# Slot-logit block sums take a turn in the two-buffer PSUM pool of the transposes, and the slot maximum is emitted at the end of its pair

## The chip, the cores and the metric

One core of a Trainium2 chip (eight cores in two dies of four) runs the whole program. The metric is the device time of that core in microseconds, as the median of several executions. Durations inside the program come from one profiled execution.

## The reference, cut to what matters

```python
scores = scale * q @ k.transpose(0, 1, 3, 2)                    # (4, 8, 576, 576)
scores = where((rel >= 0) & (rel < 128), scores + bias, -1e9)   # sliding window
attn = exp(scores - scores.max(-1)); attn /= attn.sum(-1) + 1e-9
x = (attn @ v) as (2304, 512)                                   # tokens x model
logits = x @ phi                                                # (2304, 32 slots)
d = softmax of logits over the tokens; c = softmax of logits over the slots
slot_input = d.T @ x                                            # 8 experts x 4 slots
slot_out = relu(slot_input @ w1) @ w2                           # per expert
x = c @ slot_out                                                # (2304, 512)
h = x @ w_in
out = (h * clip(h + 3, 0, 6) / 6) @ w_out
```

What the change touches is the softmax `d`, which runs over all 2304 tokens: its maximum per slot is a running one, taken block by block while the attention is still being computed.

## The kernel before

The first half, to about 176 us, is the attention stage. Its work is cut into 80 steps (batch 4, tiles of 128 tokens 5, of which the fifth has 64, pairs of heads 4). The loop at line 478 takes two steps, a "pair", at a time and emits, in the order written in `STEP` (line 30), these operations; the schedule is manual, so each engine runs its instructions in the order in which they are emitted:

- `s0 s1` (`do_s`, line 434, and `emit_s`, line 179): loads for later tiles; TensorE's score matmuls into `sp` (L190, two tiles), VectorE's bias, running minimum and row result `st` (L202), ScalarE's exponential in `pb` (L210). `do_s` also issues the loads of `q`, `k`, `v` of later tiles and of the weights on SyncE's queue; from tile 17 on (`m > 16`, line 449) it issues all weight tiles for which a buffer is free, ahead of the next `q`.
- `p0 p1` (`emit_pv`, line 241): for the two steps four back, the matmuls with `v` into `o` (L257). After the fourth step of a tile ScalarE copies `o` to `xt` (L268), and `push_tile` (line 402) appends side work.
- `b0` (`do_b`, line 472): one entry of `turnsq`, below, if it is due.
- `t0` (`emit_t`, line 228): transposes of `pb` into a tile `t` of `ps_t` (L237), two steps back; an even step's tile is copied to `xb` by VectorE, an odd one's by ScalarE (L239).
- `n0` (`emit_norm`, line 214): VectorE's reciprocal of the row sums of this pair (L217, L219) and GpSimd's multiplication of `pb` with it (L224).
- `t1`: the second transposes.
- `x0` (`do_x`, line 468): one entry of `side`: `side_x` (line 270) transposes `xt` into `xps` and ScalarE copies it to `x` (L274, L277); `side_l` (line 279) makes the slot logits `lps` and ScalarE copies them to `el` (L283, L285).

`turnsq` holds, for a block of tokens of one batch (tiles 0-1, 2-3 and 4; in the last batch tiles 0-1 and 2), three entries that are taken one per pair, the first `SLAG` = 3 steps after the block's last tile:

- `side_max` (line 289): a matmul with block identities sums the four partial logits of `el` into `lt` (L296); VectorE's maximum over it (L298) and its negation against the running one (L303); ScalarE's exponential of `lt` back into `el` (L312), the copy of 32 plain rows (L314), the factor by which older sums are rescaled (L316); VectorE's running denominator (L321), which reads that factor. The first block of all has no earlier maximum, and neither L316 nor L321.
- `side_e` (line 325): transposes of `el` into `ln` (L328), ScalarE's copy `e` (L335) and VectorE's copy into `cn` (L336). VectorE's copy is issued with a wait for ScalarE's.
- `side_s` (line 340): matmuls `ss` of `e` with `x` (L345), added to `acc` by VectorE (L351).

PSUM is full: `sp` has four banks, `ps_t` two buffers, `ps_o` one and `ps_m` one. `lt`, `ln`, `ss`, `xps` and `lps` all take that one buffer of `ps_m` in turn, and each must wait until the tile before it has been read by its last reader.

The last tiles of the last batch end differently: `last_l` (line 354) makes their logits in `sp`, and after the loop `last_max` (line 363) does maximum, exponential, transposes (`lnl`) and sums in one go. Then come the two expert products, whose weights stream in, and the second product, all unchanged.

Of the kernel before, what the change touches and what calls it, by code (L numbers as in the profile page):

```python
# [9 lines left out]
F32 = mybir.dt.float32  # L10
# [16 lines left out]
NW, NX, NY, NV, NPB = 9, 10, 2, 4, 4  # L27
LAG_T, LAG_PV = 2, 4
CMOD, CACT = 2, 1
STEP, SLAG = "s0 s1 p0 p1 b0 t0 n0 t1 x0", 3  # L30

CB = NP * 384
CX = CB + 128 + 128 + 128
# [11 lines left out]
def nq(i):  # L45
    return 128 if i < 4 else 64
# [3 lines left out]
def body(ctx: ExitStack, tc, q, k, v, phi, we, wf, cst, sel, out):  # L50
# [78 lines left out]
    with ExitStack() as a:  # L129
# [10 lines left out]
        ps_t = a.enter_context(tc.tile_pool(name="ps_t", bufs=2, space=PSUM))  # L140
        ps_o = a.enter_context(tc.tile_pool(name="ps_o", bufs=1, space=PSUM))
        ps_m = a.enter_context(tc.tile_pool(name="ps_m", bufs=1, space=PSUM))
# [127 lines left out]
        def side_x(b, i):  # L270
            w = nq(i)
            t = ps_m.tile([128, NP, 128], F32, tag="m", name=f"xps{b}_{i}")
            for j in range(NP):
                nc.tensor.transpose(out=t[0:w, j, :], in_=xt[b, i][:, j, 0:w], identity=ident)  # L274
            xn[b, i] = xp.tile([128, DM], F32, tag="x", name=f"x{b}_{i}")
            cp_ = nc.vector.tensor_copy if (b, i) == tiles[-1] else nc.scalar.copy
            cp_(out=xn[b, i][0:w].rearrange("p (j d) -> p j d", j=NP), in_=t[0:w])  # L277

        def side_l(b, i):
            w = nq(i)  # L280
            t = ps_m.tile([128, 128], F32, tag="m", name=f"lps{b}_{i}")
            for j in range(NP):
                nc.tensor.matmul(out=t[32 * j:32 * j + 32, 0:w], lhsT=phi4[:, j, 0],  # L283
                                 rhs=xt[b, i][:, j, 0:w], start=True, stop=True)
            nc.scalar.copy(out=el[:, i * 128:i * 128 + w], in_=t[:, 0:w])  # L285
# [3 lines left out]
        def side_max(b, i0, i1):  # L289
            mx = ep.tile([128, 8], F32, tag="mx", name=f"mx{b}_{i0}")  # L290
            t0, w = 128 * i0, sum(nq(i) for i in range(i0, i1))
            cuts = [(t0, w)] if w <= 512 else [(t0, w // 2), (t0 + w // 2, w // 2)]
            lt = []
            for hh, (c0, cw) in enumerate(cuts):
                t = ps_m.tile([128, 512], F32, tag="m", name=f"lt{b}_{c0}")
                nc.tensor.matmul(out=t[:, 0:cw], lhsT=blk, rhs=el[:, c0:c0 + cw],  # L296
                                 start=True, stop=True)
                nc.vector.reduce_max(out=mx[:, hh:hh + 1], in_=t[:, 0:cw], axis=AX.X)  # L298
                lt.append(t)
            nm = mx[:, 2:3]  # L300
            for hh in range(len(cuts)):
                if hh or run:
                    nc.vector.scalar_tensor_tensor(  # L303
                        out=nm, in0=mx[:, hh:hh + 1], scalar=-1.0, in1=nm if hh else run["nm"],
                        op0=ALU.mult, op1=ALU.min)
                else:
                    nc.vector.tensor_scalar(out=nm, in0=mx[:, 0:1], scalar1=-1.0, scalar2=None,
                                            op0=ALU.mult)
            z = el
            for hh, (c0, cw) in enumerate(cuts):  # L310
                zz = z[:, c0:c0 + cw]
                nc.scalar.activation(out=zz, in_=lt[hh][:, 0:cw], func=AF.Exp, bias=nm,  # L312
                                     accum_out=mx[:, 4 + hh:5 + hh])
                nc.scalar.copy(out=zz[0:32], in_=lt[hh][0:32, 0:cw])  # L314
            if run:
                nc.scalar.activation(out=mx[:, 6:7], in_=run["nm"], func=AF.Exp, bias=nm,  # L316
                                     scale=-1.0)
            if len(cuts) > 1:
                nc.vector.tensor_tensor(out=mx[:, 4:5], in0=mx[:, 4:5], in1=mx[:, 5:6], op=ALU.add)
            if run:  # L320
                nc.vector.scalar_tensor_tensor(out=mx[:, 4:5], in0=run["z"], scalar=mx[:, 6:7],  # L321
                                               in1=mx[:, 4:5], op0=ALU.mult, op1=ALU.add)
            run.update(nm=nm, z=mx[:, 4:5], al=mx[:, 6:7])
# [30 lines left out]
        def last_l(i):  # L354
            c0, w = 128 * (i - 3), nq(i)
            if i == 3:
                run["lg"] = sp[0][:, 0, 0:192]
            for j in range(NP):
                nc.tensor.matmul(out=run["lg"][:, c0:c0 + w],
                                 lhsT=phi4[:, j].rearrange("p g s -> p (g s)"),  # L360
                                 rhs=xt[B - 1, i][:, j, 0:w], start=j == 0, stop=j == NP - 1)
# [38 lines left out]
        side, turnsq = [], []  # L400

        def push_tile(n, b, i):
            if b == B - 1 and i > 2:
                side.append(lambda: last_l(i))
                side.append(lambda: side_x(b, i))
                return
            side.append(lambda: side_x(b, i))
            side.append(lambda: side_l(b, i))
            for i0, i1 in ((0, 2), (2, 3)) if b == B - 1 else ((0, 2), (2, 4), (4, NB)):
                if i == i1 - 1:  # L410
                    for f in (side_max, side_e, side_s):
                        turnsq.append((n + SLAG, lambda f=f, i0=i0, i1=i1: f(b, i0, i1)))

        nc.vector.memset(acc, 0.0)
        warm(ps_m, "m", acc, WARM_0)
# [45 lines left out]
        def do_p(n):  # L461
            m = n - LAG_PV
            if 0 <= m < NSTEP:
                emit_pv(m)
                if steps[m][2] == NP - 1:
                    push_tile(n, *steps[m][:2])
# [2 lines left out]
            if side:  # L469
                side.pop(0)()  # L470

        def do_b(n):
            if turnsq and turnsq[0][0] <= n:
                turnsq.pop(0)[1]()

        ops = {"s": do_s, "t": do_t, "n": do_n, "p": do_p, "x": do_x, "b": do_b}
        with tc.manual_schedule():
            for n in range(0, NSTEP + LAG_PV, 2):
                for c in STEP.split():
                    ops[c[0]](n + int(c[1:]))  # L480
            while turnsq:
                turnsq.pop(0)[1]()
            while side:
                side.pop(0)()
        top.close()
# [13 lines left out]
        t = ps_m.tile([128, NP, 1, NS], F32, tag="m", name="stp")  # L499
# [106 lines left out]
    with ExitStack() as bx:  # L606
# [4 lines left out]
        with tc.manual_schedule():  # L611
# [132 lines left out]
            t = ps_2.tile([128, NP, 128], F32, name="sotp")  # L744
# [66 lines left out]
    def q_out(j):  # L811
        if j < 4:
            nc.scalar.copy(out=qhi[:, j], in_=Q[j])
            nc.vector.tensor_tensor(out=qlo[:, j], in0=Q[j], in1=qhi[:, j].bitcast(F32),
                                    op=ALU.subtract)
            return
        x = tp.tile([128, DM], F32, tag="o", name="qtail")
        nc.vector.tensor_copy(out=x, in_=Q[4])
        return x
# [55 lines left out]
    with tc.manual_schedule(), tc.issue_after(L["last"].ins):  # L875
# [10 lines left out]
        for p in range(8):  # L886
# [9 lines left out]
            if last:  # L896
                x = q_out(4)
# [163 lines left out]
```

## Time and profile before

| what | us |
|---|---|
| three timed runs | 378.14, 378.93, 380.35; median 378.93 |
| the profiled execution, its own time | 379.32 |
| its span, first to last instruction | 377.4 |
| mean granted clock of TensorE (1 is 2.4 GHz) | 0.958 |
| busy: TensorE / VectorE / ScalarE / GpSimd | 336.2 / 192.3 / 178.7 / 82.3 |
| moved by DMA | 71.10 MB, mean 188 GB/s |

How to read what follows. Times are counted from the first instruction. PE is TensorE, DVE VectorE, ACT ScalarE, SPq the queue of SyncE that issues loads. A row of the timeline gives start, length, engine, line, operation and names (written<-read), the number of instructions merged, and in brackets how long the engine idled before and what ended that. A row of the list of waits gives who waited (engine, tile, line), the releaser, the time in total, how often, and the longest. The idle time of an engine counts only where that engine, or one that waits for it, is the last to finish.

### The profile page before, as it was taken

The numbers are of one execution on the slowest core, as the hardware profiler recorded it, in microseconds if no ns is written. First come the engines' busy times: TensorE is split into PE (matmuls) and PEld (weight loads), VectorE is DVE, ScalarE is ACT, GpSimd is POOL, SyncE is SP. The second block draws the span as 40 slices with busy tenths as digits, with TensorE's granted clock in tenths as the row PEclk, the third lists the DMA queues.
The fourth block names the chain that finished last, engine by engine and source line by source line (L and its number), as shares of the span: only waits on it lengthen the run. The fifth ranks groups of instructions, "written<-read, shape, count | busy, mean of one in ns | idle before, by whom it ended". The sixth has DMA issues, their size and how long they took to land. (4 is left out here: it accounts for less than half of the span.)

```text
span 377.4 us, 7557 instructions
## 1 busy us (share of the span) xinstructions
PE 336.2 (89%) x2738; PEld 205.7 (55%) x2738; DVE 192.3 (51%) x617; ACT 178.7 (47%) x551; POOL 82.3 (22%) x182
## 2 busy tenths in 40 slices
PE   6898889897989788687999685999999999999994
PEld 5566556665666556465433131433443358788883
DVE  2655465545555556224200558888888458940000
ACT  3787778777786788242021443222233045632111
POOL 2544254434443344210002200000000011110000
PEclk9999999999999999895899966999999999999999
DMA  8545784559367829177599998762000001122221
GB/s 262 198 168 199 248 325 151 212 209 361 95 215 259 329 76 411 39 240 314 196 423 391 374 425 340 243 219 97 2 0 0 2 2 56 56 83 85 83 82 64
DMA packets 19835, 71.10 MB, mean 188 GB/s; under 512 B 2672, under 2 KB 4848, under 8 KB 13776
## 3 DMA queue, kind: packets, MB, share of 16 engines
q1 hardware_dynamic: 18576, 69.08, 49.1%
q10 hardware_dynamic: 1216, 1.47, 1.2%
q8 instruction: 23, 0.38, 0.4%
q14 instruction: 20, 0.16, 0.1%
HBM read 65.83 MB, written 4.72 MB: 187 GB/s over the span
## 5 line engine op out<-in xcount | busy, mean ns | idle before, releaser
L224 POOL TENSOR_TENSOR pb<-pb,st 128x192 f32<-128x192 f32 (+2 forms) x144 | 63.6, 473 | 98.5 <-DVE st L219 45.2
L210 ACT ACTIVATE pb<-pb,st 128x192 f32<-128x192 f32 (+2 forms) x144 | 61.3, 426 | 24.8 <-DVE st L202 24.8
L805 PE MATMUL q<-F,mf 128*128 128x512 f32 x128 | 62.8, 624 | 4.3 <-DVE mf L793 4.3
L202 DVE CUSTOM_DVE_ANT_0 pb<-sp,cona 128x192 f32<-128x192 f32 (+2 forms) x144 | 40.6, 332 | 28.3 <-PE sp L190 25.8
L838 PE MATMUL acc<-qhi,P 128*128 128x512 f32 x140 | 42.1, 395 | 0.0
L257 PE MATMUL o<-xb,v 128*64 128x128 f32 (+2 forms) x576 | 41.5, 276 | 0.1
L805 PEld LDWEIGHTS q<-F,mf 128*128 128x128 f32 x128 | 23.2, 196 | 33.5 <-issue 22.3
L237 PE MATMUL t<-conp,pb 128*128 128x128 f32 x256 | 39.3, 284 | 2.0 <-POOL pb L224 1.2
L190 PE MATMUL sp<-kt,qz 64*64 64x192 f32 (+2 forms) x576 | 33.6, 318 | 4.9 <-issue 3.6
L257 PEld LDWEIGHTS o<-xb,v 128*64 128x64 f32 (+1 forms) x576 | 30.8, 138 | 12.4 <-issue 7.9
L237 PEld LDWEIGHTS t<-conp,pb 128*128 128x128 f32 x256 | 28.6, 143 | 9.5 <-POOL pb L224 5.8
L838 PEld LDWEIGHTS acc<-qhi,P 128*128 128x128 f32 x140 | 25.9, 188 | 6.1
L210 ACT ACTIVATION_READ_ACCUMULATOR pb<-pb,st 128x1 f32 x144 | 26.9, 187 | 0.0
L239 DVE COPY xb<-t 128x512 f32<-128x512 f32 (+1 forms) x40 | 23.2, 580 | 6.9 <-PE t L237 6.5
L190 PEld LDWEIGHTS sp<-kt,qz 64*64 64x64 f32 x576 | 19.6, 132 | 12.7 <-issue 8.0
L853 ACT ACTIVATE out<-acc 128x512 f32<-128x512 f32 (+1 forms) x18 | 10.6, 586 | 30.9 <-PE acc L838 23.3
L239 ACT COPY xb<-t 128x512 f32<-128x512 f32 (+1 forms) x40 | 19.7, 492 | 7.8 <-PE t L237 7.6
L795 POOL COPY mf<-mt 128x64 f32<-128x64 f32 x8 | 6.2, 774 | 78.2 <-ACT mt L785 53.2
L274 PE MATMUL xps<-conp,xt 128*128 128x128 f32 (+1 forms) x76 | 12.3, 284 | 12.3 <-ACT el L314 8.9
L777 ACT COPY m<-mp 128x256 f32<-128x256 f32 x8 | 3.0, 372 | 41.8 <-PE mp L774 41.8
L838 PE MATMUL acc<-qlo,P 128*128 128x512 f32 x56 | 22.1, 395 | 0.0
L585 DVE TENSOR_TENSOR pf<-R,As 128x512 f32<-128x512 f32 (+1 forms) x20 | 12.7, 637 | 14.1 <-ACT As L569 7.8
(153 smaller groups left out, 453.0 us busy)
## 6 DMA issues: line engine op xcount, KB each, us to landing
w<-in_we_dram SPq DMA_DIRECT2D x30, 1024.0 KB, 6.3
w<-in_wf_dram SPq DMA_DIRECT2D x16, 1024.0 KB, 8.4
out_dram<-out SPq DMA_DIRECT2D x17, 256.0 KB, 2.0
v<-in_v_dram SPq DMA_DIRECT2D x16, 256.0 KB, 3.6
qz<-in_q_dram SPq DMA_DIRECT2D x15, 256.0 KB, 5.2
kt<-in_k_dram SPq DMA_DIRECT2D x15, 256.0 KB, 5.8
kt<-in_we_dram SPq DMA_DIRECT2D x1, 1024.0 KB, 7.2
qz<-in_q_dram SPq DMA_DIRECT2D x6, 128.0 KB, 5.0
```

Source lines behind the costliest of these rows:

```text
L190: nc.tensor.matmul(out=sp[m][64 * e:64 * e + 64, hf, c0:c1], lhsT=qz[64 * u:64 * u + 64, (NB * b + i) % 2, j * w + 64 * hf:j * w + 64 * hf ...
L202: nc.vector.tensor_tensor_reduce(out=p[:, 256 * hf + c0:256 * hf + c1], in0=sp[m][:, hf, c0:c1], in1=bias8[:, j, hf, c0:c1], scale=-0.125, ...
L210: nc.scalar.activation(out=x, in_=x, func=AF.Exp, bias=st[:, 0, r], scale=-1.0, accum_out=st[:, 1, r])
L224: nc.gpsimd.tensor_tensor(out=x, in0=x, in1=st[:, 2, 2 * m + hf:2 * m + hf + 1].to_broadcast([128, c1 - c0]), op=ALU.mult)
L237: nc.tensor.transpose(out=t[:, c, hf], in_=p[:, o:o + 128], identity=ident)
L239: f(out=x[:, p0:2, 0:nh], in_=t[:, p0:2, 0:nh])
L257: nc.tensor.matmul(out=o[64 * u:64 * u + 64, j, 0:w], lhsT=vv[0:kk, 128 * j + 64 * u:128 * j + 64 * u + 64], rhs=y, start=m == 0, stop=m = ...
L274: nc.tensor.transpose(out=t[0:w, j, :], in_=xt[b, i][:, j, 0:w], identity=ident)
L585: nc.vector.tensor_tensor(out=pf, in0=t[:, 0:w], in1=(L["a2"][s % 2] if j == 4 else A[s])[:, 0:w], op=ALU.mult)
L805: nc.tensor.matmul(out=Q[pt], lhsT=mm[p][:, u, 128 * pt:128 * pt + 128], rhs=F[:, u], start=p == u == 0, stop=p == 7 and u == 1)
L838: nc.tensor.matmul(out=acc, lhsT=l, rhs=r[:, j], start=j == 0 and i == 0, stop=j == 4 and i == 1)
L853: nc.scalar.activation(out=o[:, cs], in_=acc[:, cs], func=AF.Copy, scale=1.0 / 6.0))
```

## The change

`lt` is allocated in `ps_t`, the pool of the transposes, with their tag. `STEP` gets a tenth operation, `m0`, behind `x0`. Entries of `turnsq` carry a kind: `side_max` is taken at `m0`, `side_e` and `side_s` at `b0` as before. The list stays one list: an entry is taken only if it is the first and of the kind asked for. Since `m0` comes after `b0` in a pair, a `side_max` can now follow in the pair in which the `side_s` before it was taken.

```diff
-STEP, SLAG = "s0 s1 p0 p1 b0 t0 n0 t1 x0", 3
+STEP, SLAG = "s0 s1 p0 p1 b0 t0 n0 t1 x0 m0", 3
...
-                t = ps_m.tile([128, 512], F32, tag="m", name=f"lt{b}_{c0}")
+                t = ps_t.tile([128, 512], F32, tag="t", name=f"lt{b}_{c0}")
...
-                        turnsq.append((n + SLAG, lambda f=f, i0=i0, i1=i1: f(b, i0, i1)))
+                        turnsq.append((n + SLAG, "m" if f is side_max else "b",
+                                       lambda f=f, i0=i0, i1=i1: f(b, i0, i1)))
...
-        def do_b(n):
-            if turnsq and turnsq[0][0] <= n:
-                turnsq.pop(0)[1]()
+        def do_b(n, kind="b"):
+            if turnsq and turnsq[0][0] <= n and turnsq[0][1] == kind:
+                turnsq.pop(0)[2]()
...
-        ops = {"s": do_s, "t": do_t, "n": do_n, "p": do_p, "x": do_x, "b": do_b}
+        ops = {"s": do_s, "t": do_t, "n": do_n, "p": do_p, "x": do_x, "b": do_b, "m": lambda n: do_b(n, "m")}
...
             while turnsq:
-                turnsq.pop(0)[1]()
+                turnsq.pop(0)[2]()
```

VectorE around the maximum over tiles 2-3 of the second batch, before (`mx` is the maximum, `xb<-t` the copy of a transpose, L217 and L219 the reciprocal, L202 the score reductions, here the next pair's first):

```order
L298 TENSOR_REDUCE mx_2_1270<-lt_256_1271 128x1
L303 SCALAR_TENSOR_TENSOR mx_2_1270<-mx_2_1270,mx_0_1057 128x1
L321 SCALAR_TENSOR_TENSOR mx_2_1270<-mx_0_1057,mx_2_1270 128x1
L239 COPY xb_110<-t_1279 128x256
L217 TENSOR_SCALAR st_1247<-st_1247 128x4
L219 RECIPROCAL st_1247<-st_1247 128x4
L202 ISA pb_112,st_1310<-sp_116,cona 128x192
```

and with the change:

```order
L239 COPY xb_110<-t_1270 128x256
L217 TENSOR_SCALAR st_1247<-st_1247 128x4
L219 RECIPROCAL st_1247<-st_1247 128x4
L298 TENSOR_REDUCE mx_2_1291<-lt_256_1292 128x1
L303 SCALAR_TENSOR_TENSOR mx_2_1291<-mx_2_1291,mx_0_1082 128x1
L321 SCALAR_TENSOR_TENSOR mx_2_1291<-mx_0_1082,mx_2_1291 128x1
L202 ISA pb_112,st_1310<-sp_116,cona 128x192
```

The three instructions of the maximum moved from ahead of the pair's copy and reciprocal to right ahead of the next pair's score reductions.

TensorE at the same place, before (`o` the products with `v`, `xps` the transposes of a finished tile):

```order
L257 MATMUL o_4_1214<-xb_111,v_4_848 64x64 x2
L296 MATMUL lt_256_1271<-el,conp 128x256
L237 MATMUL t_1279<-conp,pb_112 128x128 x2
L237 MATMUL t_1289<-conp,pb_113 128x128 x2
L274 MATMUL xps_4_1293<-conp,xt_4_1268 64x128 x4
L190 MATMUL sp_116<-kt,qz 64x192 x4
```

and with the change:

```order
L257 MATMUL o_4_1214<-xb_111,v_4_857 64x64 x2
L237 MATMUL t_1270<-conp,pb_112 128x128 x2
L237 MATMUL t_1280<-conp,pb_113 128x128 x2
L274 MATMUL xps_4_1284<-conp,xt_4_1268 64x128 x4
L296 MATMUL lt_256_1292<-el,conp 128x256
L190 MATMUL sp_116<-kt,qz 64x192 x4
```

The block sum `lt` moved behind the transposes `t` and `xps`, to right ahead of the next pair's scores.

TensorE at the end of the stage, where the last block's `ss`, the last logits (L359) and the last `xps` stand, before:

```order
L328 MATMUL ln_2_2357<-conp,el 128x64
L359 MATMUL sp_116<-pb_112,phi_61 128x64 x4
L345 MATMUL ss_2_2366<-x_2_2222,e_2_2359 32x128 x4
L274 MATMUL xps_4_2372<-conp,pb_112 64x128 x4
L376 MATMUL lnl<-conp,el 128x32
```

and with the change:

```order
L345 MATMUL ss_2_2362<-x_2_2213,e_2_2335 32x128 x4
L359 MATMUL sp_116<-pb_112,phi_61 128x64 x4
L274 MATMUL xps_4_2372<-conp,pb_112 64x128 x4
L376 MATMUL lnl<-conp,el 128x32
```

The last `ln` moved a pair forward, and `ss` moved from behind the last logits to ahead of them.

## Rows read from the trace of the kernel before

**Rows 1.** Stretch of the attention stage: us, busy PE, PEld, DVE, ACT, POOL, PEclk, DMA.

```profile
69.00:108.00 39.00, 34.24 (x464) 24.18 (x463) 21.89 (x117) 29.61 (x112) 15.61 (x37) 1.00 0.63 228
```

**Rows 2.** List of waits from 10 to 170 us: total, times, longest.

```profile
PE xps L274 <- ACT el L314: 8.9, 8, 1.3
...
PE lps L283 <- DVE cn L336: 3.2, 3, 1.1
...
PE xps L274 <- DVE cn L336: 1.1, 3, 0.4
...
DVE mx L321 <- ACT mx L316: 12.1, 10, 1.4
```

**Rows 3.** Timeline, the maximum over tiles 2-3 of the second batch.

```profile
83.22 0.70 PE L296 MATMUL lt<-el,conp 128*128 128x256 f32 x2
...
83.75 0.60 PE L237 MATMUL t<-conp,pb 128*128 128x128 f32 x4
...
83.90 0.35 ACT L268 COPY xt<-o 128x256 f32<-128x256 f32 x1
...
85.68 0.63 PE L274 MATMUL xps<-conp,xt 128*64 128x128 f32 x4 [1.33 <-ACT el L314]
...
85.86 0.22 DVE L321 SCALAR_TENSOR_TENSOR mx<-mx,mx 128x1 f32<-128x1 f32 x1 [1.28 <-ACT mx L316]
...
86.23 0.88 PE L190 MATMUL sp<-kt,qz 64*64 64x192 f32 x16
...
86.97 0.36 DVE L202 CUSTOM_DVE_ANT_0 pb<-sp,cona 128x192 f32<-128x192 f32 x1 [0.27 <-PE sp L190]
...
89.14 0.19 ACT L335 COPY e<-ln 128x64 f32<-128x64 f32 x1
...
89.89 0.88 PE L190 MATMUL sp<-kt,qz 64*64 64x192 f32 x16
```

**Rows 4.** Timeline, the maximum over tiles 0-1 of the second batch.

```profile
69.68 0.56 ACT L268 COPY xt<-o 128x512 f32<-128x512 f32 x1
...
71.74 0.87 PE L190 MATMUL sp<-kt,qz 64*64 64x192 f32 x8
...
75.40 0.87 PE L190 MATMUL sp<-kt,qz 64*64 64x192 f32 x8
```

**Rows 5.** The page's costliest groups: ScalarE's exponentials of the scores (mean ns).

```profile
L210 ACT ACTIVATE pb<-pb,st 128x192 f32<-128x192 f32 (+2 forms) x144 | 61.3, 426 | 24.8 <-DVE st L202 24.8
```

**Rows 6.** Timeline, the maximum over tile 4 of the second batch.

```profile
94.00 0.88 PE L190 MATMUL sp<-kt,qz 64*64 64x192 f32 x16
...
95.83 0.43 PE L296 MATMUL lt<-el,conp 128*128 128x64 f32 x2
...
97.75 0.22 DVE L321 SCALAR_TENSOR_TENSOR mx<-mx,mx 128x1 f32<-128x1 f32 x1 [1.03 <-ACT mx L316]
...
97.93 0.88 PE L190 MATMUL sp<-kt,qz 64*64 64x192 f32 x16
...
104.31 0.42 PE L345 MATMUL ss<-x,e 64*32 64x128 f32 x8
```

**Rows 7.** Timeline of SyncE's queue and of TensorE, the last tile's scores.

```profile
139.07 0.47 SPq L168 DMA_DIRECT2D v<-in_v_dram  x1
...
154.09 1.08 PE L190 MATMUL sp<-kt,qz 64*64 64x192 f32 x8 [3.61 <-issue]
...
159.07 0.87 PE L190 MATMUL sp<-kt,qz 64*64 64x192 f32 x8
```

**Rows 8.** List of waits of SyncE's queue, whole span.

```profile
SPq L110 <- DMA qz<-in_q_dram: 11.7, 1, 11.7
```

**Rows 9.** Timeline of TensorE behind the last logits.

```profile
170.26 0.66 PE L345 MATMUL ss<-x,e 128*32 128x128 f32 x8
171.38 1.06 PE L274 MATMUL xps<-conp,pb 128*64 128x128 f32 x4 [0.47 <-DVE acc L351]
```

**Rows 10.** Stretch behind the wait of 3.61 us, columns as in rows 1.

```profile
154.61:158.02 3.41, 3.41 (x26) 2.47 (x22) 0.95 (x5) 1.30 (x5) 0.00 (x0) 0.50 0.02 5
```

## The prediction

> **What bounds the kernel now.** I read the time by stretches first, then the list of waits, then the timeline around single slot maxima. In a middle stretch of the attention stage TensorE is busy 34.24 of 39 us, ScalarE 29.61, VectorE 21.89 [rows 1]. So TensorE sets the pace, and the stage is long by what TensorE waits for. The list of waits names it [rows 2]: eight times the transposes `xps` wait for the row copy of `el` (L314), 8.9 us in all, because `lt` and `xps` share the one buffer of `ps_m`. Three times `lps` waits for the copy `cn` (3.2 us), three times `xps` does (1.1 us). The same list has a wait that is hidden today: VectorE's `L321` waits for ScalarE's `L316` ten times, 12.1 us. VectorE can afford it there, since what stands behind it is only the copy of `t` and the sums of the rows.
>
> After the attention stage nothing in the program is changed, and its loads are issued as its matmuls free buffers. I therefore pass a shift of the stage's end to the end of the kernel one to one.
>
> **The change, part by part.** Instructions and DMAs are the same in number and form; no load is moved on its queue. Three things move: `lt` takes a turn in `ps_t`; the whole of `side_max` (matmul, maximum, negation, exponential, row copy, rescale factor, `L321`) goes behind `side_x`/`side_l` of its pair; and the third maximum of a batch comes one pair earlier. There are eleven maxima: four over tiles 0-1 (A), three over tiles 2-3 (B), three over tile 4 (C), one in the last batch over tile 2 (D).
>
> *What is gained, seen at B* [rows 3]. TensorE no longer issues `lt` (0.53 us, 83.22 to 83.75) ahead of the transposes, and `xps` waits only for `xt`: 83.90 + 0.35, with 0.05 that I allow for the signal, is 84.30 and not 85.68. `xps` holds TensorE 0.55, then `lt` 0.53, and the scores of the next pair start at 85.38 instead of 86.23: 0.85 gained.
>
> *What is lost, at the same B.* `L321` now stands on VectorE ahead of the next pair's four score reductions (L202), and these cannot start before it ends. The chain from `lt` to `L321` takes 85.86 - 83.22 = 2.64 us, nearly free of other work in this row, and `L321` 0.22. From the new `lt` at 84.85 that is 87.71, while L202 starts at 86.97 today: 0.74 late. On ScalarE the copy `e` stands behind the pair's exponentials, which follow L202; from L202 to `e` are 2.17 us, from `e` over `cn` to the next pair's scores 0.75. So `lps` waits longer for `cn`, and the following scores start at 90.63 instead of 89.89. **B costs 0.74**, three times. The 0.85 are lost again within the pair.
>
> *A* [rows 4]. The `xt` copy ends at 70.24, so `xps` starts at 70.29, `lt` at 70.84, the next scores at 71.37 instead of 71.74 (0.37 gained). `L321` ends at 70.84 + 2.86 = 73.70. The next tile has one half, so two exponentials of 0.43 [rows 5] fewer stand before `e`: 73.70 + 1.31 + 0.75 = 75.76 against 75.40. **A costs 0.36**. The first A has no `L321`, since there is no earlier maximum, and keeps its 0.37. The fourth lies in the wait described below and costs nothing. That leaves two.
>
> *C* [rows 6]. It now runs in the pair before. `lt` stands at 94.00; its chain to `L321` takes 97.75 - 95.83 = 1.92, so L202 follows at 96.14, `e` at 98.31 and the next scores at 99.06 instead of 97.93: 1.13 late. The two pairs behind give back the block's `ss` (0.42 long) and the `xps` wait for `cn` (0.37 of the 1.1 over three in [rows 2]), which have moved out of them. **C costs 1.13, of which 0.34 stay.**
>
> *The load that everything meets at* [rows 7, 8]. At 154.09 the scores of the last tile start after 3.61 us in which the profile names no releaser. SyncE's list shows one: its queue waited 11.7 us for a load of `qz` to land, the longest wait on a DMA in that list, and the last tile's `qz` is what these scores read. That load stands behind `v` of the last tile (issued at 139.07, when the `o` matmuls of the pair before had released a buffer) and four weight tiles. So the start at 154.09 is a load that began with TensorE's progress at 139, and moves with it. TensorE is late at that place by: first batch -0.37 + 0.74 + 0.34 = 0.71; second 0.36 + 0.74 + 0.34 = 1.44; third up to its C, 0.36 + 0.74 + 1.13 = 2.23; together **4.4**. The wait hides whatever the fourth A does.
>
> *The end of the stage* [rows 9]. The last `ss` moves one pair earlier, so `xps` follows the logits at 170.26 instead of 171.38: **-1.1**. D loses its wait (8.9 / 8 = 1.1) and gets one of B's kind: between -1.1 and 0.7, I take **-0.3**.
>
> *TensorE's clock* [rows 1, 3, 10]. It is at 2.4 GHz through the stage, also through B's waits today (at most 1.33 us), and at 1.2 GHz right after the 3.61 us. With the change TensorE idles 1.1 (today's wait of `lps` there) + 0.85 + 0.74 = 2.7 us at each B, part of it ahead of `ln`, most ahead of `lps`. No row shows a wait of that length. Its longer part, some 2.2, is nearer to the 1.33 without a fall, the two parts together nearer to the 3.61. The bounds are no fall, 0, and a fall at all three: a pair at the low clock took 159.07 - 154.09 = 4.98 [rows 7], its like at full clock 75.40 - 71.74 = 3.66 [rows 4], so 1.32 each, 4.0. I take one fall, less 0.3 for waits behind it: **1.0**.
>
> The sum is 4.4 - 1.1 - 0.3 + 1.0 = 4.0 us. The profiled execution itself took 379.32 us, 0.39 above the median of the three runs; 383.3 on its scale is **382.9** on that of the median.
>
> A rule speaks for the opposite. The Trainium skill, "Perfetto Trace Analysis", section "Matmuls" (under Optimizing Tensor Performance), wants independent matmul groups to rotate through PSUM banks, so that evacuation of one overlaps the next group. By that rule `lt` in the two-buffer pool is right and the sum would end with the gains alone. The trace agrees that the single buffer holds `xps` up [rows 2]; it also shows a second chain, through `L321`, which no PSUM buffer shortens.
>
> **The rivals.** About 0.5% (1.9 us) is what a measurement of this kernel can tell from no change.
>
> 1. *The waits go and nothing comes in their place*: L202's delay is taken up by the two `sp` tiles and four `pb` tiles. Then four A gain 0.37, three B 0.85, the end 1.1 and D 0.3: 5.4, so 373.5 us. For it speaks that VectorE is busy only 21.89 of 39; against it, that `cn` holds `lps` up already now, and everything before `cn` moves back. Chance 0.07. (This is what the rule of the page named above would give.)
> 2. *The loss is swallowed by the load* (not slower). If `qz` of the last tile lands at 154.0 however late TensorE is at 139, the 4.4 fit nearly into the 3.61, and the end gains 1.4: 378.93 - 1.4 = 377.5. It decides at the issue of the `v` load: if that stays at 139, this case holds. Against it is that this load waits for a buffer that the `o` matmuls free. Chance 0.10, no change by measurement.
> 3. *The clock falls at every B, or stays low longer*: 382.9 - 1.0 + 4.0 = 385.9. For it: the two parts of the new wait lie close together. Chance 0.16.
> 4. *Delays are half of what I add up*, because some work ahead of `e` is taken up, and no fall: about 380. Chance 0.07, no change by measurement.
>
> **How the numbers follow.** The forecast, slower through VectorE's wait with none to two falls of the clock, has 0.60 and spans 381.5 to 384.5. Slower by over 0.5%: 0.60 but for a rim of 0.01, and 0.16, gives 0.75. Within: 0.10 + 0.07 + 0.01 = 0.18. Faster: 0.07. The range leaves out rival 1, rival 2 and a little of rival 3: 379.8 to 385.6.
>
> **What would show it.** In the profile after: `xps` no longer waits for L314; `lps` waits for `cn` three times a batch (about 0.9, 2.2 and 1.3 us); `L321` waits as long as before, and L202 starts right behind it in ten pairs; a batch takes about 1.4 us more; `v` of the last tile is issued near 143.5 and the last scores start near 158.5; `xps` of the last tile follows the logits at once. I am wrong if a batch takes no longer than now, if L202 behind a maximum starts before `L321`, or if the stage ends earlier than now.

## The result and the profile after

The changed kernel takes 382.05 us (median of 20 runs, 379.27 to 384.84) against 378.49 (20 runs, 376.97 to 381.78) on the same chip. The ratio on record is 1.0078, with an interval of 1.0053 to 1.0102 (it is not the quotient of the two medians, which is 1.0094; the ratios below are of the same kind): **slower, by 2.0 to 3.9 us**. The forecast was 382.9. The profiled execution after took 380.93 us (span 379.1), that before 379.32 (377.4), so this pair of profiles shows less of the difference (1.6 us) than the medians do.

The waits of the changed kernel from 10 to 175 us (TensorE's four largest, and VectorE's `L321`):

```profile
DVE mx L321 <- ACT mx L316: 11.9, 10, 1.3
PE lps L283 <- DVE cn L336: 11.6, 8, 2.1
PE xps L274 <- ACT xt L268: 5.4, 12, 0.6
PE sp L190 <- DMA qz<-in_q_dram: 4.1, 1, 4.1
PE ln L328 <- ACT el L314: 2.2, 6, 0.4
```

The eight waits of `xps` for L314 [rows 2] are gone. The wait of `lps` for `cn` has grown from 3.2 us over three to 11.6 over eight. `L321` waits as long as before.

The timeline at the same maximum as in [rows 3], B of the second batch:

```profile
87.60 0.63 PE L274 MATMUL xps<-conp,xt 128*64 128x128 f32 x4 [0.43 <-ACT xt L268]
...
88.06 0.60 PE L296 MATMUL lt<-el,conp 128*128 128x256 f32 x2
...
88.59 0.88 PE L190 MATMUL sp<-kt,qz 64*64 64x192 f32 x16
...
90.44 0.33 PE L328 MATMUL ln<-conp,el 64*128 64x64 f32 x2 [0.39 <-ACT el L314]
90.62 0.22 DVE L321 SCALAR_TENSOR_TENSOR mx<-mx,mx 128x1 f32<-128x1 f32 x1 [1.31 <-ACT mx L316]
...
90.76 0.35 DVE L202 CUSTOM_DVE_ANT_0 pb<-sp,cona 128x192 f32<-128x192 f32 x1
...
92.92 0.19 ACT L335 COPY e<-ln 128x64 f32<-128x64 f32 x1
...
93.14 0.22 DVE L336 COPY cn<-ln 128x64 f32<-128x64 f32 x1 [1.19 <-ACT e L335]
...
93.42 0.32 PE L283 MATMUL lps<-xt,phi 128*32 128x64 f32 x8 [2.06 <-DVE cn L336]
...
93.67 0.88 PE L190 MATMUL sp<-kt,qz 64*64 64x192 f32 x16
```

`xps` waits for `xt` alone, and the next scores follow 0.53 us behind `lt`. Then the chain shows: from `lt` to `L321` 2.56 us, L202 0.14 behind it (it could have begun after the scores at 88.59), `e` 2.16 behind L202, the next scores 0.75 behind `e`.

TensorE's clock at this place, and at the other low stretches of this profile (columns as in rows 1):

```profile
89.90:94.50 4.60, 2.16 (x36) 1.31 (x32) 2.24 (x14) 3.09 (x15) 0.35 (x1) 1.00 1.00 395
94.54:97.95 3.41, 3.41 (x33) 2.66 (x32) 1.68 (x10) 2.33 (x9) 1.51 (x4) 0.50 0.72 259
...
9.21:16.04 6.83, 6.64 (x50) 3.96 (x52) 3.99 (x25) 4.23 (x19) 3.48 (x11) 0.50 0.63 230
159.39:166.22 6.83, 4.97 (x32) 3.80 (x33) 1.21 (x7) 1.31 (x5) 0.00 (x0) 0.50 0.09 34
180.07:183.29 3.22, 3.22 (x15) 3.22 (x16) 2.04 (x4) 0.57 (x1) 0.53 (x1) 0.50 0.91 310
```

From 1.1 us behind the end of the wait of B the granted clock is 0.50, that is 1.2 GHz, for 3.41 us. The same happens behind B of the first batch (53.58 to 56.99) and of the third (135.50 to 138.91). Before, none of the three showed it.

The last tile and the end of the stage, for [rows 7, 9]:

```profile
146.92 0.47 SPq L168 DMA_DIRECT2D v<-in_v_dram  x1
...
161.25 1.54 PE L190 MATMUL sp<-kt,qz 64*64 64x192 f32 x8 [4.12 <-DMA qz<-in_q_dram]
...
175.62 1.10 PE L359 MATMUL sp<-pb,phi 128*128 128x64 f32 x8 [0.17 <-ACT pb L268]
176.56 0.60 PE L274 MATMUL xps<-conp,pb 128*64 128x128 f32 x4
...
180.07 0.44 PE L501 MATMUL stp<-conp,acc 128*128 128x128 f32 x1 [0.57 <-DVE acc L394]
```

In the kernel before, the last logits (L359) and `stp` were:

```profile
168.36 1.97 PE L359 MATMUL sp<-pb,phi 128*128 128x64 f32 x8 [0.32 <-ACT pb L268]
...
175.94 0.45 PE L500 MATMUL stp<-conp,acc 128*128 128x128 f32 x1 [0.57 <-DVE acc L394]
```

`v` of the last tile moved from 139.07 to 146.92, its scores from 154.09 to 161.25; the stage's last transpose `stp` from 175.94 to 180.07.

### The profile page after: what moved, and what is told of

It is laid out like the page before. It is cut to its first block, busy times and chain, and to the rows that moved or that the text cites. A ratio compares the mean times of both kernels' runs of the same rounds, so it can differ in the third digit from the quotient of the medians.

```text
span 379.1 us, 7586 instructions
## 1 busy us (share of the span) xinstructions
PE 336.5 (89%) x2738; PEld 208.2 (55%) x2738; DVE 194.1 (51%) x617; ACT 179.3 (47%) x551; POOL 82.3 (22%) x182
## 5 line engine op out<-in xcount | busy, mean ns | idle before, releaser
L202 DVE CUSTOM_DVE_ANT_0 pb<-sp,cona 128x192 f32<-128x192 f32 (+2 forms) x144 | 40.6, 331 | 24.1 <-PE sp L190 22.7
L257 PE MATMUL o<-xb,v 128*64 128x128 f32 (+2 forms) x576 | 42.9, 283 | 0.0
L237 PE MATMUL t<-conp,pb 128*128 128x128 f32 x256 | 40.6, 300 | 1.3 <-POOL pb L224 1.3
L190 PE MATMUL sp<-kt,qz 64*64 64x192 f32 (+2 forms) x576 | 35.7, 334 | 4.8 <-DMA qz<-in_q_dram 4.1
L257 PEld LDWEIGHTS o<-xb,v 128*64 128x64 f32 (+1 forms) x576 | 31.7, 141 | 12.9 <-issue 8.4
L237 PEld LDWEIGHTS t<-conp,pb 128*128 128x128 f32 x256 | 30.0, 151 | 8.2 <-POOL pb L224 3.5
L190 PEld LDWEIGHTS sp<-kt,qz 64*64 64x64 f32 x576 | 20.4, 138 | 14.0 <-issue 5.1
L521 ACT ACTIVATE w<-w 128x1024 f32<-128x1024 f32 x16 | 18.5, 1162 | 0.0
```

The costliest lines, as they stand in the source:

```text
L190: nc.tensor.matmul(out=sp[m][64 * e:64 * e + 64, hf, c0:c1], lhsT=qz[64 * u:64 * u + 64, (NB * b + i) % 2, j * w + 64 * hf:j * w + 64 * hf ...
L202: nc.vector.tensor_tensor_reduce(out=p[:, 256 * hf + c0:256 * hf + c1], in0=sp[m][:, hf, c0:c1], in1=bias8[:, j, hf, c0:c1], scale=-0.125, ...
L237: nc.tensor.transpose(out=t[:, c, hf], in_=p[:, o:o + 128], identity=ident)
L257: nc.tensor.matmul(out=o[64 * u:64 * u + 64, j, 0:w], lhsT=vv[0:kk, 128 * j + 64 * u:128 * j + 64 * u + 64], rhs=y, start=m == 0, stop=m = ...
L521: nc.scalar.activation(out=hi, in_=hi, func=AF.Copy, scale=2.0 ** -112)
```

## The experiments

The theory: VectorE's `L321` waits for ScalarE ahead of the next score reductions, this delays the exponentials, `e` behind them, `cn`, and with `cn` TensorE. Against it stood three others: that the block sum in the two-buffer pool makes the transposes wait, that TensorE's clock costs most of it, and that the late load of the last `qz` does. Each run is compared with the kernel before on its own chip: 379.61 us (11 runs) for the first four, 379.16 (29) for the next four, 378.93 (11) for the last.

**Each half of the change alone.** The kernel before with only the pool changed, and the changed kernel with `lt` back in the single buffer:

```diff
-                t = ps_m.tile([128, 512], F32, tag="m", name=f"lt{b}_{c0}")
+                t = ps_t.tile([128, 512], F32, tag="t", name=f"lt{b}_{c0}")
...
-                t = ps_t.tile([128, 512], F32, tag="t", name=f"lt{b}_{c0}")
+                t = ps_m.tile([128, 512], F32, tag="m", name=f"lt{b}_{c0}")
```

> Half of the change: lt in the pool of the transposes, side_max still at b0. My theory (a turn in the two-buffer pool is no free buffer): lt takes the buffer that the pair's second transpose needs, so that transpose waits for the row copy L314 in place of xps; slower than the kernel before by 2 to 4 us (380.5 to 382.5), and the wait of TensorE on L314 stays, now at t. Rival (the pool is the part that helps, the order the part that hurts): xps and t are both free, 3 to 5 us faster than before (373.5 to 375.5).

> The other half: side_max at m0, lt still in the one buffer of ps_m. My theory: lt then waits for the copy of xps (or of lps), and ln, lps and xps wait for L314 behind it, on top of VectorE's delay of the full change; slower than before by 7 to 11 us (385.5 to 389.5). Rival (the order alone is what costs, the pool is indifferent): as the full change, 381 to 383.

Measured: the pool alone 385.05 us, ratio 1.0101 [1.0051, 1.0151]; the order alone 388.59, ratio 1.0244 [1.0186, 1.0303]. The list of waits of the first has a new row:

```profile
PE t L237 <- ACT el L314: 13.6, 10, 1.6
```

That of the second has these two:

```profile
PE lps L283 <- DVE cn L336: 10.4, 8, 2.1
PE lt L296 <- ACT x L277: 6.8, 10, 0.8
```

With the pool alone, `lt` still stands ahead of the pair's two transposes and takes one of their two buffers. The second transpose then waits for L314 as `xps` did, ten times instead of eight. With the order alone, `lt` takes the single buffer behind `xps` and waits for ScalarE's copy of it (L277), and the wait for `cn` comes on top. So neither half is a gain by itself. The first came out above its range (a median of 385.05 where 380.5 to 382.5 was expected), the second inside. The rule of the Trainium skill that the prediction weighed ("Perfetto Trace Analysis", section "Matmuls": rotate independent groups through banks) was followed in the first of these runs, and the wait went to the next user of the rotation.

**`L321` behind `cn`.** Nobody needs the running denominator before the next maximum, so it is deferred into `side_e`:

```diff
             if run:
-                nc.vector.scalar_tensor_tensor(out=mx[:, 4:5], in0=run["z"], scalar=mx[:, 6:7],
-                                               in1=mx[:, 4:5], op0=ALU.mult, op1=ALU.add)
+                run["late"] = lambda z=run["z"]: nc.vector.scalar_tensor_tensor(
+                    out=mx[:, 4:5], in0=z, scalar=mx[:, 6:7], in1=mx[:, 4:5],
+                    op0=ALU.mult, op1=ALU.add)
...
             run["e"] = e
+            if "late" in run:
+                run.pop("late")()
```

> The full change, but the running denominator (L321) is emitted behind cn in side_e of the next pair, so that VectorE's score reductions no longer stand behind a wait for ScalarE. My theory (VectorE's wait is the loss): L202 starts about 0.7 us earlier behind each maximum, lps waits about 1 us less at B, the clock does not fall there; a batch takes 38.5 to 39.3 us, 375 to 378 in all. Rival S (ScalarE is the loss: the next pair's exponentials stand behind the slot exponential whatever VectorE does): no change against the full change, 381 to 383.

**`e` copied by VectorE**, so that `cn` no longer waits for ScalarE's exponentials:

```diff
-                    nc.scalar.copy(out=e[0:w, a0:a1], in_=t[0:w, a0:a1, 1])
+                    nc.vector.tensor_copy(out=e[0:w, a0:a1], in_=t[0:w, a0:a1, 1])
```

> The full change, but the copy e is made by VectorE instead of ScalarE, so that e and cn no longer stand behind the pair's exponentials; L321 stays where it is. My theory (the delay reaches TensorE through e and cn alone): the waits of lps for cn shrink from 0.7, 2.1 and 1.3 us to under 0.7 each, a batch takes about 38 us, 372 to 376 in all. Rival (the delay also reaches TensorE through the scores, exponentials and GpSimd to the transposes): under 1.5 us better than the full change, new waits of t for GpSimd.

Measured: `L321` behind `cn` 373.79 us, ratio 0.9846 [0.981, 0.9881]; `e` on VectorE 370.11, ratio 0.9766 [0.9728, 0.9803]. B of the second batch with `L321` behind `cn`:

```profile
84.51 0.88 PE L190 MATMUL sp<-kt,qz 64*64 64x192 f32 x16
...
85.24 0.36 DVE L202 CUSTOM_DVE_ANT_0 pb<-sp,cona 128x192 f32<-128x192 f32 x1
...
88.17 0.19 ACT L336 COPY e<-ln 128x64 f32<-128x64 f32 x1
...
88.53 0.21 DVE L321 SCALAR_TENSOR_TENSOR mx<-mx,mx 128x1 f32<-128x1 f32 x1
...
88.67 0.32 PE L283 MATMUL lps<-xt,phi 128*32 128x64 f32 x8 [1.39 <-DVE cn L337]
```

and with `e` on VectorE:

```profile
85.53 0.22 DVE L321 SCALAR_TENSOR_TENSOR mx<-mx,mx 128x1 f32<-128x1 f32 x1 [1.31 <-ACT mx L316]
...
85.67 0.35 DVE L202 CUSTOM_DVE_ANT_0 pb<-sp,cona 128x192 f32<-128x192 f32 x1
...
86.78 0.22 DVE L335 COPY e<-ln 128x64 f32<-128x64 f32 x1
86.92 0.22 DVE L336 COPY cn<-ln 128x64 f32<-128x64 f32 x1
...
87.28 0.32 PE L283 MATMUL lps<-xt,phi 128*32 128x64 f32 x8 [0.99 <-DVE cn L336]
```

In the first, L202 starts 0.73 behind the scores instead of 2.17 (88.59 to 90.76), but `e` still waits for four exponentials, and `lps` for `cn` 1.39 us. In the second, `L321` waits as it did and L202 is as late, but `e` follows the reductions in 1.11 us instead of 2.16. Both links of the chain are real, and cutting either one makes the changed kernel faster than the kernel before. Both runs came out below what was expected (375 to 378, and 372 to 376), and a part of each gain is TensorE's clock: with `e` on VectorE it falls behind no B, with `L321` behind `cn` only behind the third. The Trainium skill says ("TensorE: Matmul & The Clock Gate", section "Architectural detail: the array is 16× 32×32, not 1× 128×128", in the passage on engine queue depths) that VectorE and ScalarE work strictly first in, first out. The two places of L202 agree: 2.17 us behind its scores where `L321` stands ahead of it, 0.73 where it does not.

**The same copy in the kernel before, and both edits in the changed one.** The first takes the edit of `e` to the old order; the second joins the two edits above.

> The kernel before, with the copy e made by VectorE; lt in ps_m and side_max at b0 as before. My theory (VectorE's wait and the row copy are apart from e): only the waits for cn go (1.1 us at B, 0.4 at C), the eight waits on L314 stay; 3 to 5 us faster than before, 374 to 376.5, and so slower than the full change with e on VectorE (0.977 of before) by 3 us or more. Rival (e was the whole matter, and pool and order add nothing once it is gone): as that kernel, 0.97 to 0.98 of before.

> The full change with both: L321 behind cn in side_e, and e on VectorE. My theory (two links of one chain, each shortening what the other leaves): a batch about 36.8 to 37.2 us instead of 37.5, no wait of lps for cn over 0.4 us; 367 to 369.5, 1 to 3 us under e on VectorE alone. Rival (with e gone from behind the exponentials TensorE is not held by VectorE's wait any more): no difference from e on VectorE alone, 0.976 of before.

Measured: `e` on VectorE in the kernel before 376.11 us, ratio 0.9916 [0.9878, 0.9954]; both edits in the changed kernel 367.75, ratio 0.9706 [0.9655, 0.9756]. From the list of waits of the first:

```profile
PE xps L274 <- ACT el L314: 8.8, 8, 1.3
...
PE lps L283 <- ACT el L314: 1.3, 3, 0.4
```

and TensorE's three largest waits in the second:

```profile
PE xps L274 <- ACT xt L268: 5.0, 12, 0.6
PE sp L190 <- DMA qz<-in_q_dram: 3.9, 1, 3.9
PE ln L329 <- ACT el L314: 2.1, 6, 0.4
```

In the old order the wait of `xps` stays at 8.8 us and the edit is worth 0.8%; in the new order, where that wait is gone, the same edit is worth some 3% (1.0078 to 0.9766), of which some 0.8% are the three falls of the clock that go with it (an estimate from the 1.05 us that each is found to cost below). Both runs lie in their expected ranges. With both edits no wait for `cn` is left, and a batch (A to A, `lt` at 67.78 and 104.41) takes 36.63 us against 39.27 before. The change removes what it was said to remove; in the batches its price is the chain through VectorE and ScalarE, with the falls of the clock behind that chain's waits.

**The clock.** Eight extra transposes at the start of the `t` of the pair behind B, into a place of the tile that the real ones overwrite, so that TensorE works where it had waited for `cn`:

```diff
+            if fill[0] and n % 2 == 0:
+                fill[0] = 0
+                for _ in range(NFILL):
+                    nc.tensor.transpose(out=t[:, 1, 0], in_=p[:, 128:256], identity=ident)
...
             run["e"] = e
+            fill[0] = (i0, i1) == (2, 4)
```

> The full change, with eight extra transposes of a row tile (written over by the right ones right after) in the pair behind each maximum over tiles 2-3, where TensorE otherwise waits about 2.1 us for cn. They add work and shorten only the idling. Clock theory (idling at B makes the granted clock fall, and the fall costs 0.6 to 0.7 us a batch beside the chain): no fall behind B, a batch 40.7 instead of 41.4, 1 to 2.5 us faster than the full change, 379.5 to 381. Rival (the fall hits matmuls that wait anyway and costs nothing): as the full change or up to 1 us slower.

Measured: 378.01 us, ratio 0.9981 [0.9944, 1.0018], below the 379.5 to 381 that were expected. TensorE at B of the second batch:

```profile
86.54 0.60 PE L301 MATMUL lt<-el,conp 128*128 128x256 f32 x2
...
89.19 1.09 PE L238 MATMUL t<-conp,pb 128*128 128x128 f32 x8
...
91.91 0.32 PE L288 MATMUL lps<-xt,phi 128*32 128x64 f32 x8 [1.18 <-DVE cn L341]
```

and the stretch around and behind it (columns as in rows 1):

```profile
90.00:96.00 6.00, 4.36 (x66) 3.13 (x65) 3.74 (x20) 4.78 (x21) 1.93 (x5) 1.00 0.95 355
```

From `lt` to `lps` it is 5.37 us, as in the changed kernel (88.06 to 93.42, 5.36): the chain is untouched, and the filler lies in the wait. The clock stays at 2.4 GHz behind all three B. From B's `lt` to the next batch's is 40.37 us (86.54 to 126.91) against 41.42 in the changed kernel and 39.26 in the kernel before (both from `lt` to `lt`). So of the 2.16 us that a batch lost, **1.05 is the clock and 1.11 the chain**.

**The load of the last `qz` ahead of the weights.** The weight tiles are asked for one key tile later:

```diff
-                    while load_next_w() and m > 16:
+                    while load_next_w() and m > 17:
```

> The full change, but SyncE's flood of weight tiles starts one tile later (m > 17), so that the last tile's q is issued ahead of it. My theory (the last scores wait for that load, whose start moves with TensorE): the wait of 4.1 us goes, the fourth maximum over tiles 0-1 costs its 0.5; 3 to 4 us faster than the full change, 378 to 379. Rival (DMA brings q no earlier, or k and weights are late instead): a wait of 2 us or more remains there or in the stage behind, under 1.5 us gained.

Measured, in the changed kernel: 377.26 us, ratio 0.9944 [0.9904, 0.9984], a little below the 378 to 379 that were expected. SyncE's queue and the last tile's scores:

```profile
147.94 0.48 SPq L168 DMA_DIRECT2D v<-in_v_dram  x1
148.47 1.17 SPq L114 DMA_DIRECT2D w<-in_we_dram  x1
149.68 0.43 SPq L161 DMA_DIRECT2D qz<-in_q_dram  x1
150.15 1.62 SPq L114 DMA_DIRECT2D w<-in_we_dram  x3
...
157.55 0.60 PE L296 MATMUL lt<-el,conp 128*128 128x256 f32 x2
...
158.08 0.87 PE L190 MATMUL sp<-kt,qz 64*64 64x192 f32 x8
```

With one weight tile ahead of `qz` instead of four, the scores follow `lt` without a wait, 3.17 us earlier, though `v` is issued 1.02 later. It is this load, behind weights on its queue, that the last scores waited for, as the prediction read from [rows 7, 8].

**All three edits together**: `L321` behind `cn`, `e` on VectorE, and the weights one tile later.

> Edit: the version with the slot maxima deferred behind `cn` and the copy `e` on VectorE, and besides the weights of the experts asked for one key tile later, so that the load of the last `qz` is not behind them. Theory: with the two first edits TensorE no longer waits on `cn`, and the only large wait left in the attention stage is the 3.9 us of the last scores on the load of `qz`; it goes, as the 4.1 us did when the same edit was made to the changed kernel alone (there the span fell from 379.1 to 376.4), and the median is 363 to 365 us. Rival: the weights now land later by as much as the load lands earlier, and the stages behind wait for them: within 1 us of the 367.75 measured without this edit. Second rival: the stage's end moves by 3 to 4 us but the clock falls at another place behind it: 366 us.

Measured: **361.83 us, ratio 0.9555 [0.9512, 0.9598]**, which beats both kernels. The last scores start at 142.03 instead of 145.56 with the first two edits alone, and the next pair's at 145.85 instead of 151.47:

```profile
142.03 0.87 PE L190 MATMUL sp<-kt,qz 64*64 64x192 f32 x8
...
145.85 0.87 PE L190 MATMUL sp<-kt,qz 64*64 64x192 f32 x8
```

It gives more than the 3.9 us of the wait, and more than was expected: a pair that had run at 1.2 GHz behind the wait (5.91 us) now takes 3.82.

## Why the prediction was right, and where its steps were not

The direction and nearly the size were right: +4.0 us forecast at the stage's end, +4.13 in the profile, +3.0 [2.0, 3.9] in the timed runs. But several terms were off, and their errors cancel. That the size came out is in part luck: 1.6 of the 4.13 us arose at the start of the program, ahead of anything the change touches, and without them the stage would end 2.5 us late. The direction is not luck; the chain that gives it went as told. Measured terms come from the starts of the score pairs in the two traces; "late" is the changed kernel's start less that of the kernel before.

| place | predicted | measured |
|---|---|---|
| first A of all | -0.37 | -0.43 |
| A, once per batch | +0.36 | +0.55 (69.51 to 78.69 is 9.18, was 66.77 to 75.40, 8.63) |
| B, three times | +0.74 | +0.49 (84.86 to 93.67 is 8.81, was 81.57 to 89.89, 8.32) |
| C, at its own pair | +1.13 | +0.85 (98.83 to 103.61 is 4.78, was 94.00 to 97.93, 3.93) |
| C, what stays | +0.34 | +0.06 |
| clock, up to the last `v` | +1.0, one fall | +3.15, three falls of 1.05 |
| last `v`, less the start of the program | 4.4 + 1.0 | 6.25 |
| last scores against last `v` | 0 | -0.7 |
| end of the stage | -1.4 | -3.0 |
| start of the program | 0 | +1.6 |

- **The chain** went link by link as predicted. From `lt` at B to `L321` 2.56 (2.64 predicted), to L202 0.14 (0.22), from L202 to `e` 2.16 (2.17), from `e` to the scores 0.75 (0.75); `lt` itself stood 3.20 behind its pair's scores (3.28). Three of these were read 0.08 too long, and that is B's difference. Waits of `lps` of 0.9, 2.2 and 1.3 us were named for A, B and C; they are 0.74, 2.06 and 1.32.
- **C** was over-estimated: its pair loses 0.85, of which the two pairs behind give back 0.79, as much as was said.
- **The clock** is the step that failed. The prediction had a fall at every B as rival 3, and took one fall instead, "less 0.3 for waits behind it". It fell at all three, and the filler run prices each at 1.05, not the 1.32 read from [rows 4, 7]. Rival 3's own time (385.9) also lay outside the range, which ended at 385.6 and was said to leave out only a little of that rival. That time still did not come, because the chain cost about 1.3 us less up to the last `v` (6.25 - 3.15 = 3.1 instead of 4.4) and the end gained more.
- **The load**: `v` moved by 7.85 us and the scores by 7.16, so the load moved with TensorE, as the forecast said and rival 2 denied. Run with the load ahead of the weights, the wait is gone.
- **The end of the stage**: the 3.0 us are a sum of three parts. The pair of the last scores, right behind the fourth A, lost 0.74 (5.72 us, was 4.98), where the prediction had nothing; low clock covers 4.97 us of it instead of the 3.41 of [rows 10]. Up to the last logits 0.64 were gained (5.76, was 6.40), where D was put at 0.3. From the last logits to `stp` 3.13 were gained (4.45, was 7.58): 1.1 of them is the last `ss`, as predicted (`xps` follows the logits with no `ss` between), and the other 2 go with the clock: the kernel before ran all of this at 1.2 GHz (its L359 lasted 1.97 us, now 1.10), the changed one at 2.4. No run holds the clock fixed there.
- **The pass-through**, one to one, did not hold in this pair of profiles. Of 4.13 us at `stp`, 1.7 are left at the end of the span. The kernel before spends 19.6 us behind `stp` at 1.2 GHz (5.98, 6.83 and 6.83), the changed one 13.5 (3.22, 3.42 and 6.83), and TensorE was busy in 17.8 and 10.7 of them, so the clock can account for up to half of 7.1 us. In the nine edited kernels the shift at `stp` and that of the span differ by -2.5 to +0.6 us, at shifts between -17 and +12: one to one holds within 2.5 us, and what makes the rest was looked at in this one pair alone. A forecast of this size needed that as a bound.
- Rival 1, gains and nothing in their place (373.5), is met or passed as soon as the chain is cut at one link: 373.79 and 370.11.

What stays open: which part of the wait at B the clock answers to, the 0.39 us ahead of `ln` or the 2.06 ahead of `lps`; why like waits brought a fall in one batch and not in another (last section); and how much the fourth maximum's pair and D gained for themselves, since both lie beside low clock.

## What to carry to other kernels

When an instruction is moved to the end of a stage's turn, read what is behind it on every in-order engine it uses: a tiny instruction that waits (here 0.22 us of work behind 1.3 us of waiting) stops a whole next turn if the turn's first work stands behind it, and costs nothing if it stands where nobody waits. A buffer that is freed moves the wait to the next user of the rotation, so follow the chain to the tile that TensorE waits for next, and cut it there before judging the change. Price a falling clock per place and not per kernel, allow for its coming at one turn and not at the next, and look for the prefetches that stand ahead of the one load that is late.

## What the runs showed of the hardware that was not expected

- TensorE fell to 1.2 GHz behind waits of 0.39 and 2.06 us with work between them, at every B, also in the run with the weights one tile later, while the waits of 0.74 at A, 1.32 at C and 1.33 at B in the kernel before [rows 3] left it at 2.4 GHz in the two profiles compared. Eight transposes put into the wait (0.39 and 1.18 us left) kept it up, and were worth 3.7 us by the two ratios (1.0078 to 0.9981).
- Shorter waits are not safe either. With `L321` behind `cn`, TensorE waited 0.39 and 1.38 us at each B, and the clock fell behind the third alone. With `e` on VectorE in the kernel before, `xps` waited 1.32 us at each B, as it does in the kernel before itself, and the clock fell at the first alone. The two stretches, in that order (columns as in rows 1):

```profile
127.60:131.01 3.41, 3.41 (x42) 2.08 (x35) 1.78 (x10) 2.37 (x10) 1.90 (x4) 0.50 0.97 371
...
46.40:49.81 3.41, 3.26 (x28) 2.06 (x28) 1.98 (x11) 1.89 (x7) 1.26 (x4) 0.50 0.96 317
```

- The profile after has 6.83 us of low clock at its start (9.21 to 16.04), where the instructions are those of before, whose profile has none there; the fifth pair of scores starts at 18.82 instead of 17.22. So 1.6 us of a single profile's difference can lie in a place that the change does not touch.
